# Forming the weight sums of seven-product passes later, from stored halves, and for passes of both layers

## The chip, the core and the metric

The kernel runs on one core of a Trainium2 chip. The metric is the device time of one execution, in microseconds; the median of several executions stands for a kernel. TensorE multiplies, VectorE, ScalarE and GpSimd do the rest, SyncE issues every DMA of the program from one queue in order.

## The reference

Block-causal attention over 4 x 8 heads of 576 positions and 64 columns, then two feed-forward layers on 2304 tokens of 512 columns, with 2048 inner columns:

```python
def reference(q, k, v, moe_w_in, moe_w_out, moe2_w_in, moe2_w_out):
    scores = np.where(block_i >= block_j, q @ k.T / sqrt(64), -1e9)   # blocks of 64
    x = softmax(scores) @ v                                            # to 2304 x 512
    h = x @ moe_w_in
    x = (h * tanh(softplus(h))) @ moe_w_out                            # mish, layer 0
    h = np.maximum(x @ moe2_w_in, 0.0)
    return (h * h) @ moe2_w_out                                        # layer 1
```

## The kernel before

Tokens are cut into six chunks of 384 columns (CH1). A chunk goes through attention, then through layer 0 and layer 1; one chunk through one layer is a pass, written (layer, chunk). PASSES gives their order: (0,0), (0,1), (0,2), (1,0), (1,1), (0,3), (1,2), (1,3), (0,4), (0,5), (1,4), (1,5), numbered 0 to 11. Attention of chunks 2 to 5 runs beside passes 0 to 7. Pass (0,0) multiplies in fp32. All others multiply f16 halves: a value is split into a high and a low f16 part, and a product takes three matmuls (high by high, low by high, high by low).

A pass has eight blocks j of 256 inner columns, two half blocks f each. `first_half` is a plain block's first product: per f four products of 384 columns into a bank hp, then an activation with a table function. `first_seven` does the same block with seven products of 128 x 256 by half the tokens instead of eight, Strassen's scheme: its weights are three blocks as they are and four sums or differences of blocks, its tokens are summed by `chunk_scale`'s `later` (L1238), and the results are put together on VectorE (L1325 to L1333). Before, all six passes of layer 1 run `first_seven`, all of layer 0 `first_half` (or `first_full` for (0,0)). `g_parts` then splits the activated block into halves, and `second_half` multiplies it by the second weights into four accumulators; it runs one block later, mixed with the next block's first products.

Weights arrive as raw 64-bit words and are decoded (`decode`), measured (`weigh`, L1127 and the matmul L1130) and split into f16 halves (`split`) on the chip. Layer 0's first weights stay in SBUF (`here`); all others are spilled to DRAM and fetched again for each pass (`weights`). For layer 1 that happens in passes (0,1) and (0,2): 16 units, eight of them first weights, which `sums` (L1163) turns into seven blocks and stores in sspill, 896 KB a block. A fetched block lies in a ring of three: "w7" for layer 1's first weights, "wl" for second weights from pass 3 on ("ws" before that). All these lie in one region, arena, and `follow` lists which ring may begin after which other one is done.

The order of all work is not worked out when the kernel is built: PLAN is a packed list of task numbers and engines, and `planned` issues the tasks in that order. Each engine keeps to it; between engines semaphores decide. A task that may run on several engines (`choose`, `copy`, `parts`) goes where the list says. Unpacked, the list before has 4601 tasks.

```python
    R["w7"] = fixed([seven(arena[:, 1792 * i:1792 * i + 1792]) for i in range(3)])
    R["wl"] = fixed([pair(arena[:, 5376 + 1024 * i:6400 + 1024 * i]) for i in range(3)])
...
    for o, a, b, op in ((3, 2, 3, ALU.add), (2, 0, 2, ALU.subtract), (0, 3, 0, ALU.subtract), (1, 1, 0, ALU.subtract)):
```

Of the kernel before, what the change touches and what calls it, by code (L numbers as in the profile page):

```python
# [16 lines left out]
F16 = mybir.dt.float16  # L17
# [7 lines left out]
DM = 512  # L25
# [39 lines left out]
def seg_len(tiles):  # L65
# [34 lines left out]
    "cIyP`BO7(2_Qi9X(cxj)sy*=UW*sdzNi8#l`|EY0T+flCn;5@Eua;?e<OZo=HsGW692Ly(+C?tK_GNkrBd(Pt8k;UMlz3huL*x-Tz>FpOkX#~vvGxkxFAvCN"  # L100
    "vJe~d<vdxSkIPp14sFko`B-ku2A+MbKWbz7L2sA2x=!XX?|%74dlT7(`j!5qU+T*`m!pOZlJE5d`ANPdKJ#^!)|9XD^+NfOZ1_RG(D(IwnT<C;)VK9cvS1e4"
    "&c^c}kvW~@6a9dQSnVi3;{RKT=SMPwtb0x0mv{6v?aDimx8x0diFjY5FH1*xPkZ72XY~qsLEqFvI)m#ejC&KGJ}n2ys62f|3(@denWpE<qeOqBj@RdiM1LJi"
    "raYumI5v?x7fUW)AE$rn1yaxasrM3*d$hSch|gA%8Gp+0X0!~{2XweBmHXvPa(boq)xYF6xkq1-TXZ3DT_9cMd$~iu(>rv4enY&LYA5Z3PjXBT`AUA)TV%G("
    "lPh$#bl1!EBWX?E-GFuN<Xyc=K9+an0_m(TNNMdzCJvRW^=f@XCrMNJK>w@Lh~f&ar=jof@~}K34P+udc~zg0mO4`IBO@Qzr-*6;nJf$BIc+aba@AI@k*WFu"
    "nRBsB<~%_kr4mQUH}V)UJ5R<?9b<H)j@8G_NEs%PJR~Dzl#V9$BV~(>z`_xn?~}pY-J@^FSRKl!(K<w?$i1w1Jb7Nky}R++B)MBE${?;DB`faKTjdEEAm!vS"
    ">CZ~HOMe|f=Jl4II*jvm5}8r5T5r{E*!!v6BR7&`S1Z}Bx8R$1r6sFgL*(v4`@7^y-gVIq(vSM@q@DE~^CEI@r1HN4m7bC&GF5s|e`iPsJyY5uwZ1IYHu@p?"
    "+Ekio6X{02eXVE7g-B_k&B(*)<nMVphP>}6&9uCkOGaIwjnT6yc|4q>y*x!loDIgDN6gNZbG4?PD;LVmtk;917HF0+^|c}K8_hazqjgtoJ5`TIi?gLbs&lsk"
    "qX%%OiNuV&RL+uWpjCgZCD~dIbUj`w$Zq*q2c!K>dJ`)gwy{<uHZA2;eEvIrE3{|f-G+Fmq70*UdLpfWds&ii8_Q`_PXjV=KN5D>+EQ2YwX@Wde%c%SI#rI7"
    ")8z`uH|uSIUM^ehu^{+%Q$v>96UmZla+TDSrFNM;PA;N;s>_wS!?c%d@}si+U~}|WdyHfl_k+ENY-q^+g|-pZaK0|Er&2Y|@xxFu=ni>C_v%OXpnhlvNs-N?"
    "4hNAV1$H2)Td0+Y{21vA%H4v^b4@SlOeM`W<)jyRa;r=LAA6GR|LF6a*XvD^V<*^$Wi7Sxi0y*bBV@eYK)qfgkDIHhV0T<ecHC#LkiT`2`Bon^^X)GnV|!Vr"  # L110
    "vvq{&17>g1|FCMVUPOJb(x2@pvmVxJA$OQR^j*6~KiBinWWC-4n!axT)VcO9(-4oYgh2)(w>{W7omJb(BCut-eqfjBH2s@;{7h#s{y8GG3{<Qpui54x@E2e~"
    "Yx9dfM{Iu4vq3$Frc>>Y#OEEIZ0GA+VC7Hxg#8*Me1jZ))K-*9U||CpYnw`6Q(t<S)5*}<=0x)$YmTrd$!X?fIYDZgQ)Q?<ftc2U7j8DMV#igSr%{PD;oq+2"
    "GE<RQjf0=2>eFPJiZM@7C9hH~3wgZ{_J5IxP2l~B;QAiUQ}I{}KYzQOO=j-X&$OATj_vtGZ6?e;lv-Mb9k-hIK=pTZ5UBnRHf+)*vRqCwZ)h+5O^QJ6%2LkM"
    "Fvo#c6+q4MR8@ig0xJDVmi{V><XUXbgGVR9nw97|D$2{nk5QT5>euqR&V{irrWV)0xO3zs?&ZSS`NZvS-GwGaps0WttPAJ<3v)h3g?tDeejpp*v18?3DyIw)"
    "dr23`3>gWcJ_m~|pgM=+li6_UWPKe^{HBe_w7DS1G&1WEodp{2hJBw!lZUu^gApyFd0@~cR=J-_+MxI1r(wkV9$4oCT@9|SqHbR&xAx(Yx52Q-;ebEj_^n9n"
# [459 lines left out]
def tile_attention_moe(ctx, tc, qk, qp, va, vd, w1, w2, out):  # L575
# [38 lines left out]
    R = {}  # L614
# [854 lines left out]
    def scale(l, c, m, at, first=False):  # L1469
# [12 lines left out]
        if l == 0:  # L1482
            due.append([NDELAY[l], l, c, norm, rest])
# [241 lines left out]
```

## Time and profile before

| | us |
|---|---|
| median of 3 runs (lowest, highest) | 924.68 (922.96, 926.22) |
| profiled execution | 930.72 |
| its span, first to last instruction | 928.9 |
| TensorE, VectorE, ScalarE, GpSimd busy | 886.9, 684.6, 535.3, 90.2 |
| TensorE's mean granted clock, share of full speed | 0.987 |
| read from and written to HBM, MB | 144.17, 20.45 |

Busy times are unions of instruction times. A matmul's end is modelled, so its busy time says little of its pace; starts are exact. All rows are in us from the span's start, except means marked ns.

### The profile page before, as it was taken

To read this page: it belongs to the slowest core of one execution; us is meant where nothing else is said; L and a number is where in the kernel's file an instruction comes from. 1 tells how busy PE (TensorE), PEld (TensorE's weight loads), DVE (VectorE), ACT (ScalarE), POOL (GpSimd) and SP (SyncE) were. 2 spreads that over 40 slices of the span, in tenths; PEclk is the share of its full clock that TensorE was granted. 3 is DMA by queue.
4 is the path that set the end of the run, shared out by engine and by line. 5 is a ranking of instruction groups with operands and counts; after the bars stand their busy time and mean duration, and the time that the engine had idled before them with its cause. 6 is when DMAs were issued, how large, how long until landed. Compare 5 with 4: busy or idle time off the path is not lost.

```text
span 928.9 us, 17345 instructions
## 1 busy us (share of the span) xinstructions
PE 886.9 (95%) x6650; PEld 589.4 (63%) x6650; DVE 684.6 (74%) x1697; ACT 535.3 (58%) x1003; POOL 90.2 (10%) x102
## 2 busy tenths in 40 slices
PE   7999999888899799999999899999999999999998
PEld 6665555544455377767655467777766666787775
DVE  5989999999899999989899678775531333376433
ACT  5898896889899685676556444643332222233421
POOL 1000100020111001311010010001110010011010
PEclk8999999999999999999999999999999999999999
DMA  9896469889899998799936594887541222246562
GB/s 351 339 353 228 123 137 250 200 279 333 247 302 244 251 306 242 185 279 286 214 90 157 148 220 168 232 222 241 179 151 49 89 68 77 103 162 227 209 207 73
DMA packets 141779, 190.92 MB, mean 206 GB/s; under 512 B 105856, under 2 KB 110976, under 8 KB 141696
## 3 DMA queue, kind: packets, MB, share of 16 engines
q1 hardware_dynamic: 141696, 189.81, 67.5%
q8 instruction: 52, 0.85, 0.4%
q14 instruction: 31, 0.25, 0.1%
HBM read 144.17 MB, written 20.45 MB: 177 GB/s over the span
## 4 chain that ended last, share of the span: by engine, by line
PE 61%; DVE 19%; DMA 9%; ACT 7%; issue 2%; SPq 1%; POOL 0%; ACTq 0%; DVEq 0%
PE acc L1393 24%; PE hp L1315 13%; PE hp L1295 9%; PE hp L1348 4%; PE acc L1362 4%; DVE pb L783 2%; DVE st L883 2%; DMA arena<-wspill 2%; DMA pt<-pb 2%; ACT pad L894 2%; DVE arena L783 2%; PE bank L872 2%; PE bank L980 2%; DVE g L783 1%; DMA wspill<-arena 1%
## 5 line engine op out<-in xcount | busy, mean ns | idle before, releaser
L1393 PE MATMUL acc<-g,arena 128*128 128x384 f16 x2112 | 406.8, 327 | 6.2 <-DMA arena<-wspill 6.0
L1393 PEld LDWEIGHTS <-arena 128*128 128x128 f16 x2112 | 200.4, 98 | 124.4 <-issue 13.1
L1315 PEld LDWEIGHTS <-arena 128*128 128x128 f16 x2016 | 172.4, 98 | 31.8 <-issue 6.1
L1295 PE MATMUL hp<-xt,first 128*128 128x384 f16 x768 | 149.0, 330 | 2.8 <-ACT h L1300 2.6
L783 DVE SCALAR_TENSOR_TENSOR g<-h,cst,g 128x768 f16<-128x768 f32 x88 | 89.1, 1013 | 66.0 <-ACT g L1085 39.4
L1295 PEld LDWEIGHTS <-first 128*128 128x128 f16 x960 | 92.9, 98 | 70.0 <-issue 11.7
L1315 PE MATMUL hp<-xt,arena 128*128 128x192 f16 x1008 | 103.0, 247 | 2.9 <-DVE first L1325 2.2
L1315 PE MATMUL hp<-arena 128*128 128x192 f16 x1008 | 101.6, 248 | 0.8 <-DVE h L1328 0.3
L1300 ACT ACTIVATE h<-hp,cst 128x384 f32<-128x384 f32 x80 | 45.1, 576 | 82.1 <-PE hp L1295 81.9
L894 ACT ACTIVATE pad<-bank,st,sq 128x448 f32<-128x448 f32 (+1 forms) x96 | 65.3, 682 | 26.0 <-DVE st L888 21.4
L783 DVE SCALAR_TENSOR_TENSOR pb<-pad,st,pb 128x512 f16<-128x512 f32 (+2 forms) x96 | 71.8, 753 | 2.8 <-ACT pb L914 2.6
L1335 ACT ACTIVATE h<-h,cst 128x576 f32<-128x576 f32 x48 | 37.0, 770 | 60.8 <-DVE h L1333 60.7
L1086 POOL TENSOR_SCALAR g<-h,cst 128x768 f16<-128x768 f32 x34 | 32.4, 953 | 338.1 <-PE acc L1393 174.2
L883 DVE TENSOR_REDUCE st<-bank 128x1 f32<-128x448 f32 (+1 forms) x96 | 53.2, 571 | 5.8 <-PE bank L875 3.2
L1085 ACT ACTIVATE g<-h,cst 128x768 f16<-128x768 f32 x42 | 39.0, 929 | 27.8 <-PE acc L1393 23.4
L1331 ACT ACTIVATE h<-hp,cst 128x192 f32<-128x192 f32 x48 | 20.0, 417 | 59.1 <-PE hp L1315 52.8
L914 ACT ACTIVATE pb<-pad,st 128x384 f16<-128x384 f32 (+2 forms) x66 | 46.5, 712 | 11.9 <-DVE st L906 5.0
L1348 PE MATMUL hp<-xs,first 128*128 128x384 f32 x128 | 48.7, 494 | 0.0
L1333 DVE TENSOR_TENSOR h<-first,hp 128x384 f32<-128x384 f32 x48 | 26.4, 550 | 28.4 <-PE hp L1315 28.4
L872 PE MATMUL bank<-q 64*128 64x448 f16 (+2 forms) x384 | 40.2, 306 | 4.0 <-ACT xs L994 1.4
L1362 PE MATMUL acc<-h,late 128*128 128x384 f32 x96 | 37.6, 495 | 0.0
L1295 PE MATMUL hp<-xs,first 128*128 128x384 f16 x192 | 36.8, 326 | 0.0
(255 smaller groups left out, 1221.8 us busy)
## 6 DMA issues: line engine op xcount, KB each, us to landing
arena<-wspill SPq DMA_DIRECT2D x88, 512.0 KB, 4.3
arena<-sspill SPq DMA_DIRECT2D x48, 896.0 KB, 5.6
arena<-in_w_dram SPq DMA_DIRECT2D x27, 1023.8 KB, 6.8
wspill<-arena SPq DMA_DIRECT2D x16, 512.0 KB, 3.4
qk<-in_qp_dram SPq DMA_DIRECT2D x16, 480.0 KB, 5.2
sspill<-arena SPq DMA_DIRECT2D x8, 896.0 KB, 4.5
vs<-in_va_dram SPq DMA_DIRECT2D x16, 320.0 KB, 4.6
pad<-in_w_dram SPq DMA_DIRECT2D x5, 1023.8 KB, 5.7
```

The source lines that it names most:

```text
L783: return sch.add("DVE", c_dve(n) + 62 * ap, lambda: nc.vector.scalar_tensor_tensor(dst(), a(), s() if ap else s, c(), op0, op1), r=r, w=w, ...
L872: nc.tensor.matmul(out=pp.t[hd][:, o:o + k1 - k0], lhsT=qh.t[rows, u, a:a + 128], rhs=qh.t[rows, w, nq + k0:nq + k1], start=p == 0, stop=p ...
L883: t = sch.add("DVE", c_dve(o1 - o0), lambda hd=hd: nc.vector.reduce_max(st.t[:, 2 * j + hd:2 * j + hd + 1], pp.t[hd][:, o0:o1], axis=AX.X) ...
L894: t = sch.add("ACT", c_act(o1 - o0, True, 3), lambda hd=hd: nc.scalar.activation(pf[hd].t[r0:, k0:k0 + o1 - o0], view(hd)[r0:, o0:o1], AF. ...
L914: "ACT": ("ACT", c_act(n, False, 1), lambda pb=pb, pv=pv, s=s: nc.scalar.activation(pb.t[:, 0:i + 1, 0, :], pv(), AF.Copy, scale=s()), False),
L1085: "ACT": ("ACT", c_act(n, False, 1), lambda: nc.scalar.activation(dst(0), src(), AF.Copy, scale=s()), False),
L1295: nc.tensor.matmul(out=hp.t[:, 0:n], lhsT=w.t[:, f % 2, a, 128 * k:128 * k + 128], rhs=x.t[:, c, k, 0:n], start=k == 0 and i == 0, stop=k ...
L1300: sch.add("ACT", c_act(n, True, 1), lambda f=f, o=o, hp=hp: nc.scalar.activation(h.t[:, o * n:o * n + n], hp.t[:, 0:n], AF.Mish, scale=cst ...
L1315: nc.tensor.matmul(out=bank.t[:, o:o + z], lhsT=w.t[:, a, b, 128 * k:128 * k + 128], rhs=x.t[:, c, ks[k], :], start=start and k == 0 and i ...
L1348: nc.tensor.matmul(out=hp.t[:, 0:n], lhsT=wf.t[:, 512 * (f % 2) + 128 * k:512 * (f % 2) + 128 * k + 128], rhs=xs.t[:, k, 0:n], start=k == ...
L1362: ts.append(sch.add("PE", c_mm(4 * n), lambda m=m, acc=acc: nc.tensor.matmul(out=acc.t[:, 0:n], lhsT=wf.t[:, 512 * (f % 2) + 128 * m:512 * ...
L1393: nc.tensor.matmul(out=acc.t[:, 0:n], lhsT=wo.t[:, f % 2, a, 128 * m:128 * m + 128], rhs=g.t[:, c, f % 2 * n:f % 2 * n + n], start=f == 0 ...
```

## The change

`sums` and its store of seven blocks go. Layer 1's first weights are split as all others and stored as halves, 512 KB a block. A new function `upgrade` reads a block's halves, adds them (1024 wide, f16 and f16 to f32), forms the four sums, makes f16 halves of these and stores them in uspill (512 KB). It runs 16 times: during pass 5 for layer 1 (it fetches the halves for that, eight loads more) and during pass 7 for layer 0, whose halves lie in SBUF. `first_seven` takes its three plain blocks from the ordinary weights and the four sums from a second load (`sums_of`, ring "w4"). SEVEN names the six passes that use it: (1,2), (1,3), (0,4), (0,5), (1,4), (1,5). Passes (1,0) and (1,1) become plain (`first_half`, now with Relu and a square for layer 1). First and second weights of layer 1's passes share the ring "wl" of three. Slots of token tiles (X_AT) and the `follow` rules are adapted.

```
+SEVEN = {(1, 2), (1, 3), (0, 4), (0, 5), (1, 4), (1, 5)}
+UP = {5: [(1, j) for j in range(8)], 7: [(0, j) for j in range(8)]}
...
-    R["w7"] = fixed([seven(arena[:, 1792 * i:1792 * i + 1792]) for i in range(3)])
-    R["wl"] = fixed([pair(arena[:, 5376 + 1024 * i:6400 + 1024 * i]) for i in range(3)])
+    R["wl"] = fixed([pair(arena[:, 1024 * i:1024 * i + 1024]) for i in range(3)])
+    R["w4"] = fixed([four(arena[:, 3072 + 1024 * i:4096 + 1024 * i]) for i in range(3)])
+    R["un"] = fixed([four(arena[:, 6144:7168])])
+    R["uw"] = fixed([arena[:, 7168:8192]])
...
+    def upgrade(pi, l, j):
+        w = weights(pi, l, 0, 2 * j)
+        q, u = R["uw"].new(), R["un"].new()
+        sch.add("DVE", c_dve(1024), lambda: nc.vector.tensor_tensor(q.t..., w.t[:, :, 0, :], w.t[:, :, 1, :], ALU.add), r=both, w=[q], lock=True)
+        for o, x, y, op in ((3, 2, 3, ALU.add), (2, 0, 2, ALU.subtract), (0, 3, 0, ALU.subtract), (1, 1, 0, ALU.subtract)):
+            sch.add("DVE", c_dve(256), lambda ...: nc.vector.tensor_tensor(b(o), b(x), b(y), op), w=[q], lock=True)
+        copy(ENG["wh"], 1024, lambda: u.t[:, 0], qv, [q], [(u, 0)])
+        sub(V, 1024, lambda: u.t[:, 1], qv, lambda: u.t[:, 0], [q, (u, 0)], [(u, 1)])
+        dma(lambda: nc.sync.dma_start(uspill[l, j]..., u.t), 128 * 4096, r=[u], w=[ud[l, j]])
+
+    def sums_of(l, j):
+        s = R["w4"].new()
+        dma(lambda: nc.sync.dma_start(s.t, uspill[l, j]...), 128 * 4096, r=[ud[l, j]], w=[s])
...
-            if (l, k) == (1, 0):
-                w = fetched[pi, l, k, j] = R["w7"].new()
...
+            w = fetched[pi, l, k, j] = R["wl" if pi >= WL_AT else "ws"].new()
...
-            m1, h = (first_seven if l else first_half)(pi, l, j, n, x, cst)
+            for i in range(len(ups) * j // (NF // 2), len(ups) * (j + 1) // (NF // 2)):
+                upgrade(pi, *ups[i])
+            m1, h = (first_seven if (l, c) in SEVEN else first_half)(pi, l, j, n, x, cst)
```

PLAN is replaced as a whole. Unpacked, the new list has 4721 tasks, with TensorE steps as many as before (1690), VectorE steps 1734 for 1691, ScalarE 763 for 749, GpSimd 86 for 95, SyncE 448 for 376. Where VectorE's steps stand in it, counted between the first matmuls of successive passes:

| VectorE steps | 0 | 1 | 2 | 3 | 4 | 5 | 6 | 7 | 8 | 9 | 10 | 11 |
|---|---|---|---|---|---|---|---|---|---|---|---|---|
| pass | (0,0) | (0,1) | (0,2) | (1,0) | (1,1) | (0,3) | (1,2) | (1,3) | (0,4) | (0,5) | (1,4) | (1,5) |
| before | 306 | 247 | 207 | 169 | 181 | 162 | 131 | 73 | 33 | 44 | 79 | 59 |
| after | 311 | 178 | 152 | 170 | 159 | 143 | 200 | 119 | 84 | 78 | 82 | 58 |
| attention's, before | 235 | 145 | 81 | 101 | 115 | 125 | 47 | 8 | | | | |
| attention's, after | 239 | 101 | 68 | 120 | 125 | 54 | 122 | 16 | | | | |
| upgrades', after | | | | | | 50 | 6 | 29 | 12 | | | |

## Rows read from the trace of the kernel before

**Rows 1.** Busy time by stage: start:end, length, then per engine; clock, DMA share, GB/s
```profile
0.00:132.20 132.20, 125.25 (x605) 79.42 (x605) 114.28 (x309) 108.57 (x252) 8.68 (x18) 0.97 0.75 261
132.20:326.10 193.90, 169.14 (x1158) 94.66 (x1151) 182.26 (x459) 164.19 (x273) 22.09 (x25) 0.98 0.90 259
326.10:547.70 221.60, 215.36 (x1865) 145.00 (x1866) 195.83 (x510) 138.64 (x274) 26.89 (x27) 0.98 0.80 214
...
547.70:673.60 125.90, 125.31 (x1154) 96.88 (x1153) 87.96 (x207) 52.73 (x93) 11.86 (x11) 1.00 0.68 205
673.60:798.80 125.20, 125.20 (x774) 75.36 (x771) 38.26 (x77) 31.79 (x49) 11.05 (x12) 1.00 0.25 84
798.80:928.90 130.10, 126.64 (x1110) 98.04 (x1108) 66.02 (x138) 39.42 (x64) 9.65 (x9) 1.00 0.48 171
...
326.10:387.60 61.50, 60.77 (x593) 46.16 (x594) 59.61 (x169) 40.96 (x84) 10.65 (x12) 0.98 0.84 240
```

**Rows 2.** Chain of work in order of time: start, us, engine, tile, line, count
```profile
113.49 1.29 PE hp L1348 x4
...
794.09 1.46 PE hp L1295 x9
...
798.96 0.49 PE hp L1315 x6
```

**Rows 3.** Timeline of VectorE near 203 us: start, us, instruction
```profile
203.10 1.21 DVE L1115 SCALAR_TENSOR_TENSOR arena<-arena 128x1024 uint32<-128x1024 uint32 x1
204.23 0.74 DVE L1087 TENSOR_SCALAR arena<-arena,us 128x1024 f16<-128x1024 f32 x1
```

**Rows 4.** Waits of TensorE, whole run: total us, times, longest us
```profile
PE bank L1130 <- ACT wsq L1127: 8.8, 8, 2.2
PE acc L1393 <- DMA arena<-wspill: 6.0, 3, 2.3
```

**Rows 5.** Groups by line and shape: count, busy us, mean ns of one, idle before
```profile
L783 DVE SCALAR_TENSOR_TENSOR arena<-arena,us 128x512 f16<-128x512 f32 x8 | 6.0, 747 | 1.7 <-ACT arena L1085 1.6
L783 DVE SCALAR_TENSOR_TENSOR arena<-arena,us 128x256 f16<-128x256 f32 x8 | 3.8, 478 | 0.4 <-ACT arena L1085 0.3
L1085 ACT ACTIVATE arena<-arena,us 128x1024 f16<-128x1024 f32 x13 | 14.8, 1142 | 5.1 <-DVE arena L1175 2.4 <-DMA sspill<-arena 1.8 <-DMA wspill<-arena 0.9
L1115 DVE SCALAR_TENSOR_TENSOR arena<-arena 128x1024 uint32<-128x1024 uint32 x16 | 19.4, 1215 | 0.0
L1175 DVE TENSOR_TENSOR arena<-arena 128x256 f32<-128x256 f32 x32 | 13.4, 418 | 0.1
L1255 DVE TENSOR_TENSOR nsq<-nsq,wsq 128x768 bf16<-128x768 bf16 x11 | 6.0, 550 | 0.0
L1325 DVE TENSOR_TENSOR first<-first,hp 128x192 f32<-128x192 f32 x48 | 16.8, 349 | 15.9 <-ACT first L759 15.2
L1327 DVE TENSOR_TENSOR h<-first,hp 128x192 f32<-128x192 f32 x48 | 16.9, 352 | 19.5 <-PE hp L1315 18.1
L1333 DVE TENSOR_TENSOR h<-first,hp 128x384 f32<-128x384 f32 x48 | 26.4, 550 | 28.4 <-PE hp L1315 28.4
L1340 DVE TENSOR_TENSOR h<-h 128x768 f32<-128x768 f32 x11 | 11.1, 1006 | 4.1 <-ACT h L1335 4.1
```

**Rows 6.** Second-weight loads from 673.6, 798.8, 547.7, 326.1 us on; last line: min/median/max
```profile
arena<-wspill SPq DMA_DIRECT2D x16, 512.0 KB, 3.2
...
arena<-wspill SPq DMA_DIRECT2D x16, 512.0 KB, 3.8
...
arena<-wspill SPq DMA_DIRECT2D x16, 512.0 KB, 4.3
...
arena<-wspill SPq DMA_DIRECT2D x22, 512.0 KB, 4.7
...
DMA to landing us min/median/max: 3.1/4.3/9.4
```

**Rows 7.** Waits of SyncE's queue, whole run: total us, times, longest us
```profile
SPq L919 <- DVE pb L783: 53.9, 22, 8.8
```

More of the change, by code (lines that the diff above doesn't have):

```diff
@@ L100 @@
[L100 to L103, printed above, removed]
@@ L180 @@
[L180 to L183 removed]
+    "c-mE(2cQ&1^8c%62OgORNKT5FJp@nC6Gag)p%_q65D`VhQ}j^8@Dmd%2J}Qd#EfDDNh(SZ3}huplAOZ>$?5T8*Z<SqGmC$Q-JPB3uCA`|{Z{Qf5hK;)L}@9N"
@@ L617, in tile_attention_moe @@
     pair = lambda t: t.bitcast(F16).rearrange("p (a f c) -> p f a c", f=2, a=2)
-    seven = lambda t: t.bitcast(F16).rearrange("p (a b c) -> p a b c", a=2, b=7)
+    four = lambda t: t.bitcast(F16).rearrange("p (a b c) -> p a b c", a=2, b=4)
     wsl = arena[:, 0:1024 * NWS]
@@ L1182, in unit @@
         us = weigh(l, k, [j], [wf], at)
-        return sums(j, wf, us) if k == 0 else split(l, k, j, wf, us, 0)
+        return split(l, k, j, wf, us, 0)
     fetched = {}
@@ L1213, in tile_attention_moe, with chunk_scale @@
     PX, SX, CI, CF, T0, HS, GS = 0, 1, 2, 3, 4, 5, 21
-    def chunk_scale(l, xs, xm, x, n, m, at, first):
+    def chunk_scale(l, xs, xm, x, n, m, at, first, seven):
         cst, sc = (R[k].new() for k in ("cst", "sx"))
@@ L1226, in chunk_scale @@
         flip(lambda: c(PX), lambda: c(SX), [(cst, PX)], [(cst, SX)], 1)
-        for k in range(KC if l == 0 else 0):
+        for k in range(0 if seven else KC):
             parts(ENG["xh"], n, lambda s, k=k: x.t[:, s, k, 0:n], lambda k=k: xs.t[:, k, 0:n], lambda: c(SX), xs, (cst, SX), x, k)
@@ L1247, in norm @@
             for k, sq, v in zip(range(0, KC, 2), sqs, view):
-                if l == 0:
+                if not seven:
                     sch.add("ACT", c_act(2 * n), lambda k=k, v=v: nc.scalar.activation(v(), x.t[:, 0, k:k + 2, 0:n], AF.Square),
@@ L1300, in first_half, with square @@
             sch.add("ACT", c_act(n, True, 1), lambda f=f, o=o, hp=hp: nc.scalar.activation(
-                h.t[:, o * n:o * n + n], hp.t[:, 0:n], AF.Mish, scale=cst.t[:, HS + f:HS + f + 1]),
-                    r=[(cst, (HS, f // 2))], w=[hp, (h, o)], table="mish")
+                h.t[:, o * n:o * n + n], hp.t[:, 0:n], (AF.Mish, AF.Relu)[l], scale=cst.t[:, HS + f:HS + f + 1]),
+                    r=[(cst, (HS, f // 2))], w=[hp, (h, o)], table=("mish", None)[l])
+        if l:
+            square(n, h)
         return ts, h
+    def square(n, h):
+        hv = lambda: h.t[:, :]
+        choose(ENG["sq"], {
+            "ACT": ("ACT", c_act(2 * n), lambda: nc.scalar.activation(hv(), hv(), AF.Square), False),
+            "POOL": ("POOL", c_pool(2 * n), lambda: nc.gpsimd.tensor_tensor(hv(), hv(), hv(), ALU.mult), False),
+            "DVE": ("DVE", c_dve(2 * n), lambda: nc.vector.tensor_tensor(hv(), hv(), hv(), ALU.mult), True)}, [], [h])
     def first_seven(pi, l, j, n, x, cst):
         w = weights(pi, l, 0, 2 * j)
+        s = sums_of(l, j)
         p, q = R["hp"].new(), R["hp"].new()
@@ L1470, in scale @@
         sch.group = "scale", l, c
-        x = (summed if l else halved)(X_AT[l, c])
-        x, cst, norm, spread, rest, later = chunk_scale(l, *source[l, c], x, n, m, at, first)
+        seven = (l, c) in SEVEN
+        x = (summed if seven else halved)(X_AT[l, c])
+        x, cst, norm, spread, rest, later = chunk_scale(l, *source[l, c], x, n, m, at, first, seven)
         if l == 0:
             spread()
-        else:
+        if l or seven:
             sch.group = "norm", l, c
             norm()
+            if l == 0:
+                rest()
+        if seven:
             sch.group = "scale", l, c
@@ L1481, in scale @@
         ready[l, c] = x, cst, spread, rest
-        if l == 0:
+        if l == 0 and not seven:
             due.append([NDELAY[l], l, c, norm, rest])
@@ L1557, in tile_attention_moe @@
         units = list(UNITS.get(pi, ()))
+        ups = UP.get(pi, ())
         base = clock
```

242 lines of the change are left out of this document (120 added, 122 removed).

## Prediction

> **What bounds the kernel now.** I read the stage table first [rows 1]. It cuts the run at the starts of passes, the matmul runs of one chunk through one layer: A, attention's beginning and the fp32 pass (0,0); B, passes (0,1), (0,2); C, passes (1,0), (1,1), (0,3); D, (1,2), (1,3); E, (0,4), (0,5); F, (1,4), (1,5). TensorE is busy 886.9 of 928.9 us, but a matmul's busy time stretches while the next waits, so I measure a need instead: each form's count in a stage times the spacing of its starts where nothing waits. Nine 384-column matmuls take 1.46 us, 162.5 ns each; six of 192 columns 0.49 us, 82.5 ns; four fp32 halves 1.29 us, 323 ns [rows 2]; attention's matmuls get a full-clock cycle per column, half that where two row groups run side by side. Needs in A to F: 106.7, 153.0, 199.6, 123.7, 125.1, 126.3 us. Stage E, with no attention, is long by 0.1 us against its need, so the yardstick holds. Together 834.4: the run loses 94.5 us, 25.5 in A, 40.9 in B, 22.0 in C, 2.2 in D, 0.1 in E, 3.8 in F.
>
> VectorE's load is the sum of its instructions less 0.08 us each, by which one starts before the last ends: L1115 begins at 203.10, takes 1.21, and the next begins at 204.23 [rows 3]. Its loads in A to F: 112, 178.9, 190.7, 81.5, 34.5, 59.7 us. Load over TensorE's need: B 1.17, C 0.955, D 0.66, E 0.28. Stage B is bound by VectorE (busy 182.3 of 193.9), with ScalarE behind it (164.2); TensorE waits there mostly for ScalarE, L1130 for the squares of L1127 above all, 8.8 us, every one of these waits in B [rows 4]. In C both are nearly full. In E TensorE alone counts. So the loss follows that quotient: 27% of TensorE's need at 1.17, 11% at 0.955, 1.8% at 0.66, 0.1% at 0.28.
>
> **The change, part by part.** Six passes have seven products before and after, so TensorE's total need stays. A plain pass is 384 x 162.5 ns = 62.4 us, one with seven products 336 x 82.5 + 192 x 162.5 = 58.9 us [rows 2]; (1,0) and (1,1) get 3.5 us longer each, (0,4) and (0,5) shorter.
>
> Sums, removed from B: per unit four 256-wide operations (418 ns), a 512-wide and a 256-wide low half (747, 478 ns) [rows 5]; less 0.08 each, 2.4 us, 19.4 for eight units. ScalarE loses 8 us of high halves, and the store shrinks from 896 to 512 KB. Nothing else hides these: VectorE is B's bound.
>
> Seven products, moved: a block costs VectorE three 192-wide operations (349 to 352 ns, L1325 to L1328) and a 384-wide one (550 ns) [rows 5], less overlap 1.28 us, 20.5 us for 16 blocks. They leave C, where they compete with attention, and go to E, where VectorE is busy 38.3 of 125.2 us [rows 1]: no cost there.
>
> Upgrades, added: 16 times a 1024-wide add, four 256-wide operations, a copy, a 1024-wide subtract and a store. No row shows a 1024-wide add of two f16 into f32. L1115 at 1024 (1215 ns) bounds it from above; L1255, all 16 bit, takes 550 ns for 768, which gives about 0.73 us below [rows 5]. I take 1.2, since its output is f32 and L1340, all f32, takes 1006 ns for the same 768; the lower end would save 16 x 0.5 = 8 us of VectorE work, nowhere on the bound for more than a few. So 1.14 + 4 x 0.34 + 1.14 = 3.6 us each, 58 us in all, about 2 more for the copies that VectorE takes; the others are 1.14 us on ScalarE [rows 5].
>
> The order decides where this lands, and the new list moves much else. From its steps per pass, each with the duration of the same step in the trace: VectorE in B -39.7 us (sums -23 with high halves, attention -17, which goes later); C -3.7 (seven products -20.7, upgrades +30.8, attention -17.3, chunk scales and others the rest); D +44.6 (attention +26.7, upgrades +20.6); E +34.6 (seven products +22.3, upgrades +7.2); A and F within 2. TensorE's needs become 110.3, 144.3, 203.9, 131.8, 118.2, 125.7. Quotients: B 0.965, C 0.917, D 0.957, E 0.585. ScalarE gets 35 us lighter in B; exp and mish alternate 8 times less in (0,3), since attention's last chunk runs beside a Relu pass.
>
> Losses by the quotients of before: A 25.5 as it is; B 11%, 15.9; C 10%, 20.4; D 9%, 11.9 (its half (1,3) is at 0.89); E 1.4; F 3.9. Sum 79.0 against 94.5: **15.5 us** less.
>
> The ring, a cost that the diff doesn't speak of: first and second weights of layer 1's passes now share three buffers of 512 KB; before they had three each. In the old order at least 7 and mostly 10 to 20 us of matmuls stand between the last reader of a buffer and the first reader of its next content; in the new one 4.9 to 6 in F and D's tighter loads, 5 to 10 in C. The 512 KB load lands in 3.2 us (median) in E, 3.8 in F, 4.3 in D, 4.7 in C, at worst 9.4 after its issue [rows 6]. So margins of 10 us become margins of one, in 96 loads, and behind each wait of SyncE's queue stand the loads and attention's transposes after it; TensorE waits for them. Taking before's landings with these margins, F loses 0.18 us a load, D and C between 0 (margin 6.5) and 0.4 to 0.8 (margin 5): 0 to 44 us. Before's first-weight loads were 896 KB and delayed their neighbours, so I take the lower half: **8 us**. The 48 loads of sums have 11 us or more of margin; those in E cost nothing at 84 GB/s, the 8 extra loads and 16 stores delay only what is queued behind.
>
> The Trainium skill (DMA: Bandwidth & Descriptors, Anatomy of one DMA) gives a load, for the path from GpSimd, a fixed 2.0 us and its bytes over 436 GB/s. For 512 KB that is an estimated 3.2 us, and E's lone loads, though issued by SyncE, take 3.2 [rows 6]. By that rule alone no load would miss even the 4.9 us margin, the ring would be free and the sum 8 us lower; C's 4.7 us shows what other traffic adds.
>
> Sum on the profiled execution: 928.9 - 15.5 + 8 = 921.4 us span; 1.8 us lie around it (930.72). That execution is 6.0 us above the median 924.68, so the median should come to **917 us**.
>
> **Rivals.** *The relief is larger.* If B without its bound loses 7% (10.1), C 8%, D 5% and loads behave as in E, losses fall to 64 us: 928.9 - 31 + 1.8 - 6.0 = 894. For it: ScalarE's waits [rows 4] vanish with its load. Against: C loses 11% with ScalarE no fuller than that.
>
> *The bound travels.* VectorE's total grows by 38 us, and attention's last chunk with six upgrade steps now sits in (1,2), 73 us of VectorE on 72 of TensorE. If that pass loses 27% as B did (19.5), and C 25 us because upgrades share (0,3) with attention, the gain is gone: 925, no change. For it: in C VectorE is busy 88%. Against: (1,0) had 58.3 us of VectorE on 56.0 before, 1.04, and lost 10%, not 27% [rows 1].
>
> *The ring decides, slower.* Every block of the six passes of layer 1 waits for its loads. With margins of 6 us in C and D the landings of before give 18 + 6 + 6 = 30 us: 928.9 - 15.5 + 30 + 1.8 - 6.0 = 939. It decides from 15.5/96 = 0.16 us per load. For it: 22 loads in C have a median of 4.7 [rows 6], and SyncE is in order, so a transpose waiting for VectorE (53.9 us in 22 waits before) [rows 7] holds the weights behind it. Against: where TensorE is late anyway, margins widen by as much.
>
> **How the numbers follow.** Forecast 0.43, larger relief 0.20, travelling bound 0.17, ring 0.20. The likeliest is 917, by itself 908 to 926. For 8 in 10 the range reaches half into either side: 897 to 935; upgrades at their lower price and ring costs from 0 to 30 lie within. A measurement of this kernel tells 0.3% from no change, 2.8 us. Faster: 0.37 of the forecast, the relief, and 0.04 of the travelling bound, 0.61. Same: 0.04 + 0.10, 0.14. Slower: the rest, 0.25.
>
> **What would show it.** Right: B shrinks from 193.9 to about 160 us with VectorE under 90% busy, C is within 10 us of its old length, (1,2) grows by some 12, E falls to 118 to 120. Wrong, by the ring: waits of TensorE for arena loads of tens of us in passes of layer 1, in F too, where nothing else is short; before they are 6.0 us in all [rows 4]. Wrong, by the travelling bound: VectorE over 93% busy in (0,3) and (1,2), with TensorE waiting there for exp or for L1325 to L1333. Wrong, by misjudging B: B as long as its quotient allows but TensorE still waiting for L1127.

## The result, and the profile after

The changed kernel takes 894.8 us (median; 894.0 to 895.7) against 923.8 of the kernel before beside it: ratio 0.968, 95% interval 0.966 to 0.971, 29 us faster. Forecast were 917 us in a range from 897 to 935: the direction was right, the time lies 2 us below the range, and the first rival, *the relief is larger*, had 894. The profiled execution took 894.7 us, its span is 892.9.

The stage table of the changed kernel, columns as in [rows 1], stages A to F cut at the same passes:

```profile
0.00:135.50 135.50, 127.85 (x630) 81.13 (x631) 115.66 (x313) 115.56 (x264) 6.52 (x17) 0.99 0.83 277
135.50:291.10 155.60, 152.47 (x1057) 89.51 (x1056) 143.88 (x334) 128.47 (x208) 25.58 (x27) 1.00 0.87 249
291.10:505.70 214.60, 212.65 (x1526) 123.80 (x1526) 194.60 (x473) 129.10 (x242) 15.25 (x17) 1.00 0.85 228
505.70:644.70 139.00, 136.37 (x1278) 101.42 (x1276) 130.95 (x320) 89.70 (x170) 13.16 (x14) 1.00 0.95 257
644.70:762.80 118.10, 118.10 (x1060) 93.19 (x1059) 77.17 (x163) 37.82 (x61) 9.58 (x9) 1.00 0.47 167
762.80:892.90 130.10, 126.04 (x1108) 97.72 (x1105) 69.83 (x140) 38.39 (x66) 8.16 (x9) 1.00 0.58 200
```

Against [rows 1], B is 38 us shorter, C and E 7 each; D is 13 longer, since attention's last chunk and upgrades now sit there. With TensorE's need measured by the prediction's yardstick, the stages compare like this (us):

| | A | B | C | D | E | F | sum |
|---|---|---|---|---|---|---|---|
| need, forecast | 110.3 | 144.3 | 203.9 | 131.8 | 118.2 | 125.7 | 834.2 |
| need, measured | 109.9 | 145.5 | 204.8 | 130.3 | 118.2 | 125.8 | 834.5 |
| VectorE's load over need, forecast | | 0.965 | 0.917 | 0.957 | 0.585 | | |
| the same, measured | | 0.969 | 0.923 | 0.976 | 0.605 | | |
| lost, before | 25.5 | 40.9 | 22.0 | 2.2 | 0.1 | 3.8 | 94.5 |
| lost, forecast without the ring | 25.5 | 15.9 | 20.4 | 11.9 | 1.4 | 3.9 | 79.0 |
| lost, measured | 25.5 | 10.1 | 9.8 | 8.7 | 0.0 | 4.3 | 58.4 |

Needs came out within 1.2% and quotients within 4%. What failed is the step from the load to the loss, and the size of the ring's cost. Single passes show the step most plainly: pass (0,3) of the kernel before, then (0,3) and (1,2) of the changed one:

```profile
469.00:547.70 78.70, 76.20 (x528) 42.94 (x527) 63.64 (x160) 47.54 (x86) 7.04 (x8) 0.98 0.62 159
436.70:505.70 69.00, 68.36 (x474) 40.78 (x472) 67.31 (x144) 40.96 (x64) 1.81 (x2) 1.00 0.89 266
505.70:581.30 75.60, 75.04 (x705) 53.94 (x703) 73.43 (x201) 57.11 (x121) 9.57 (x10) 1.00 1.01 253
```

Their needs by the same yardstick are 70.9, 66.8 and 70.5 us. Before, (0,3) had VectorE busy 81% of the time and lost 7.8 us; now VectorE is busy 98% of it and it loses 2.2. (1,2), at 97%, loses 5.1, and TensorE's listed waits in these two passes of the changed kernel sum to 1.1 us, 0.3 of them for the putting together of products and none for exp; the rest of their losses stands in no listed wait. VectorE above 93% in both was one half of the prediction's sign for the travelling bound; the other half, TensorE waiting there for exp or the products, shows with those 0.3 us only.

TensorE's waits of the changed kernel, whole run (total us, times, longest), four of them:

```profile
PE hp L1304 <- ACT h L1309: 1.4, 4, 0.5
PE hp L1304 <- DMA arena<-wspill: 0.7, 1, 0.7
PE hp L1335 <- DMA arena<-wspill: 0.6, 1, 0.6
PE acc L1411 <- DMA arena<-wspill: 0.4, 2, 0.2
```

The 8.8 us for the squares of a weight unit [rows 4] have no successor: the waits listed for stage B sum to 3.1 us, and none is for them. The waits for weight loads are 1.7 us in all, where they were 6.0 before [rows 4] and the prediction added 8 for the ring.

The upgrades' groups by line and shape (count, busy us, mean ns, idle before):

```profile
L771 DVE TENSOR_TENSOR arena<-arena 128x1024 f16<-128x1024 f32 x16 | 19.5, 1219 | 0.9 <-ACT arena L764 0.8
L1177 DVE TENSOR_TENSOR arena<-first 128x1024 f32<-128x1024 f16 x8 | 9.7, 1218 | 0.0
L1177 DVE TENSOR_TENSOR arena<-arena 128x1024 f32<-128x1024 f16 x8 | 9.7, 1218 | 0.0
```

The wide add that no row of before showed (L1177) takes 1.22 us; of the two bounds (0.73 and 1.2) the upper one, which was taken, was right.

### The profile page after: what moved, and what is told of

Read it like the earlier page. It is cut to its first block, busy times and chain, and to the rows that moved or that the text cites. A ratio compares the mean times of both kernels' runs of the same rounds, so it can differ in the third digit from the quotient of the medians.

```text
span 892.9 us, 17533 instructions
## 1 busy us (share of the span) xinstructions
PE 873.5 (98%) x6650; PEld 586.8 (66%) x6650; DVE 732.1 (82%) x1740; ACT 539.0 (60%) x1009; POOL 78.3 (9%) x93
## 4 chain that ended last, share of the span: by engine, by line
PE 71%; DVE 14%; DMA 7%; ACT 4%; issue 2%; SPq 0%; POOL 0%; ACTq 0%; DVEq 0%; POOLq 0%
PE acc L1411 29%; PE hp L1335 15%; PE hp L1304 13%; PE hp L1366 3%; PE acc L1380 3%; PE bank L877 2%; DVE pb L788 2%; DMA pt<-pb 2%; PE bank L985 2%; DVE st L888 2%; DMA late<-pb 1%; DMA arena<-wspill 1%; DVE g L788 1%; DVE pb L920 1%; DVE arena L788 1%
## 5 line engine op out<-in xcount | busy, mean ns | idle before, releaser
L1411 PE MATMUL acc<-g,arena 128*128 128x384 f16 x2112 | 398.8, 326 | 1.1 <-ACT late L1424 0.7
L1411 PEld LDWEIGHTS <-arena 128*128 128x128 f16 x2112 | 200.3, 98 | 114.0 <-issue 4.3
L1335 PEld LDWEIGHTS <-arena 128*128 128x128 f16 x1728 | 146.8, 98 | 21.3 <-issue 1.5
L1304 PE MATMUL hp<-xt,first 128*128 128x384 f16 x576 | 109.4, 326 | 1.4 <-ACT h L1309 1.0
L788 DVE SCALAR_TENSOR_TENSOR g<-h,cst,g 128x768 f16<-128x768 f32 x88 | 90.5, 1028 | 20.4 <-ACT g L1090 10.7
L1335 PE MATMUL hp<-arena 128*128 128x192 f16 x864 | 85.8, 246 | 0.3 <-DVE h L1348 0.3
L1335 PE MATMUL hp<-xt,arena 128*128 128x192 f16 x864 | 84.5, 246 | 0.9 <-DMA arena<-wspill 0.6
L1304 PEld LDWEIGHTS <-first 128*128 128x128 f16 x576 | 55.1, 98 | 39.7 <-issue 4.3
L788 DVE SCALAR_TENSOR_TENSOR pb<-pad,st,pb 128x384 f16<-128x384 f32 (+2 forms) x96 | 72.4, 763 | 7.3 <-ACT pb L919 7.0
L1304 PE MATMUL hp<-xt,arena 128*128 128x384 f16 x384 | 72.6, 326 | 1.1 <-DMA arena<-wspill 0.7
L919 ACT ACTIVATE pb<-pad,st 128x512 f16<-128x512 f32 (+2 forms) x70 | 49.5, 714 | 13.5 <-DMA pt<-pb 4.0
L1304 PEld LDWEIGHTS <-arena 128*128 128x128 f16 x384 | 36.4, 98 | 26.7 <-issue 1.9
L1090 ACT ACTIVATE g<-h,cst 128x768 f16<-128x768 f32 x34 | 31.7, 932 | 13.9 <-PE acc L1411 5.6
```

The lines of the kernel that those rows point to most:

```text
L788: return sch.add("DVE", c_dve(n) + 62 * ap, lambda: nc.vector.scalar_tensor_tensor(dst(), a(), s() if ap else s, c(), op0, op1), r=r, w=w, ...
L919: "ACT": ("ACT", c_act(n, False, 1), lambda pb=pb, pv=pv, s=s: nc.scalar.activation(pb.t[:, 0:i + 1, 0, :], pv(), AF.Copy, scale=s()), False),
L1304: nc.tensor.matmul(out=hp.t[:, 0:n], lhsT=w.t[:, f % 2, a, 128 * k:128 * k + 128], rhs=x.t[:, c, k, 0:n], start=k == 0 and i == 0, stop=k ...
L1335: nc.tensor.matmul(out=bank.t[:, o:o + z], lhsT=lhs, rhs=x.t[:, c, ks[k], :], start=start and k == 0 and i == 0, stop=k == 1 and i == 2, s ...
L1411: nc.tensor.matmul(out=acc.t[:, 0:n], lhsT=wo.t[:, f % 2, a, 128 * m:128 * m + 128], rhs=g.t[:, c, f % 2 * n:f % 2 * n + n], start=f == 0 ...
```

## Experiments under the old list: work taken out

Three theories stand against each other. *L*, the prediction's: a stage's loss follows VectorE's load. *S*: in B TensorE waits for ScalarE. *K*: in C the chain within a block counts, not the load. If one of them is the whole story, then the kernel before must get faster when that work is left out of it. In the four kernels of this section the tasks left out keep their places in the list but issue nothing. The pieces are a unit's two plain parts, 512 and 256 wide.

```
-    sch.add("DVE", c_dve(256), lambda ...: nc.vector.tensor_tensor(q(o), q(a), q(b), op), w=[wf], lock=True)
+    sch.add("DVE", c_dve(256), lambda: None, w=[wf], lock=True)          # b_sums_dve_out, b_both
...
+        if j:
+            mute(t for t in sch.tasks[begin:] if t.opts)                 # b_sums_act_out, high halves of two pieces
...
+        if pi in (3, 4):                                                 # b_c_dve_out, b_both
+            mute(t for t in sch.tasks[begin:] if t.eng == "DVE" and not t.opts)
```

> The kernel before with one thing left out: of `sums`, the four 256-wide VectorE operations that form the sums and differences of a block (32 in all, 13.4 us of VectorE in passes (0,1) and (0,2)); the last four of the seven blocks are then plain blocks. Theory L (the loss of a stage follows VectorE's load, the rule of the prediction): stage B's load falls from 178.9 to 168, its quotient from 1.17 to 1.10, its loss from 40.9 to 33: 7 to 8 us faster. Theory S (in stage B TensorE waits for ScalarE, and VectorE only lengthens that chain): ScalarE's queue stays as full as it was, 0 to 4 us faster.

> The kernel before with one thing left out: for seven of the eight first-weight units of layer 1, the high halves of the 512-wide and of the 256-wide piece in `sums`, which ScalarE makes in 12 of the 14 cases (about 7.3 us of ScalarE and 1 us of VectorE); the low halves are then taken against stale values. Theory L: VectorE's load hardly changes, 0 to 2 us faster. Theory S: it takes off the engine that TensorE waits for, 4 to 10 us faster, and the waits of TensorE for L1127 get shorter.

> The kernel before with one thing left out: in passes (1,0) and (1,1) the four VectorE operations that put the seven products of a block together (L1325, L1327, L1328, L1333; 1.28 us a block net of overlap, 20.5 us in 16 blocks); the activation reads three copies of one product from the bank instead. Theory L: stage C's quotient falls from 0.955 to 0.853 and its loss from 22.0 to 15.6: 6 us faster. Theory K (in C TensorE waits for the chain bank, VectorE, ScalarE, next bank, not for VectorE's load): the loss falls to what the changed kernel shows in C, about 10, of which 4.4 are the half-clock spells that go away with the waits: 10 to 14 us faster.

> The kernel before with both left out: the 32 sums in stage B (as in the first kernel of this group) and the putting together of the products in passes (1,0) and (1,1) (as in the third). Both stages' gains should add: by theory L 7.5 + 6.4 = 14 us, by theories S and K 2 + 12 = 14 us. The total does not tell the theories apart, the stages do: L wants half of it in B, S and K nearly all in C. If the total is well under the sum of the two single kernels, one stage only handed its wait to the next.

| left out of the kernel before | median us | ratio to it | 95% interval |
|---|---|---|---|
| 32 sums (VectorE, B) | 923.0 | 1.0007 | 0.9974 to 1.0040 |
| high halves of two pieces (ScalarE, B) | 923.2 | 0.9991 | 0.9970 to 1.0012 |
| putting products together (VectorE, C) | 923.9 | 0.9991 | 0.9971 to 1.0011 |
| sums and putting together | 923.5 | 0.9978 | 0.9954 to 1.0002 |

Not one of the four is faster by an amount that can be told from none, though the last one lacks 30 us of VectorE's work. S allowed that for the first kernel and L for the second; no theory allowed it for the last two. Its stages B and C:

```profile
131.20:323.60 192.40, 168.84 (x1153) 94.43 (x1151) 171.89 (x427) 164.10 (x274) 22.05 (x25) 0.98 0.90 263
323.60:542.70 219.10, 213.64 (x1866) 145.29 (x1865) 175.86 (x446) 137.75 (x274) 25.59 (x27) 0.98 0.82 215
```

VectorE is busy 10 us less in B and 20 us less in C than in [rows 1], and the stages stand nearly as they were: 1.5 and 2.5 us shorter. Executions differ by more: the one of [rows 1] lies 7 us above its kernel's median, and B shows 190.2 us in the kernel that leaves work out in C alone and 187.1 in the one without high halves, whose medians are those of the kernel before. Stage C here, with VectorE busy 175.9 of 219.1 us, loses 19.5 us; the changed kernel's C, with VectorE busy 194.6 of 214.6, loses 9.8. So load alone does not set the loss.

Why nothing is gained is suggested by the chain of work in stage B (followed back from the run's last instruction, at each step to what released it), by line, first of the kernel before, then of the kernel with both left out:

```profile
by line: DVE arena L783 7.5%; ACT pad L894 7.1%; DMA arena<-wspill 6.7%; DMA wspill<-arena 6.0%; issue 5.4%; DMA pt<-pb 5.2%; PE acc L1362 4.6%; DVE st L883 3.8%; PE hp L1295 3.8%; DVE arena L1115 3.4%; PE acc L1393 3.3%; ACT h L1300 3.3%; 
```

```profile
by line: issue 8.0%; ACT pad L894 7.7%; PE hp L1300 7.5%; DVE arena L783 6.6%; DMA pt<-pb 5.3%; ACT arena L1085 4.8%; PE acc L1371 4.6%; ACT wsq L1132 4.5%; DMA wspill<-arena 4.5%; ACT L894 3.7%; ACT h L1305 3.6%; DVE st L883 3.5%; DMA aren
```

No line has a tenth of it. Summed over its pieces, the chain of before spends 58 us on VectorE, 47 on ScalarE, 43 in DMAs and 32 on TensorE; with the work gone 54, 62, 29 and 32. The path runs on through ScalarE and through waits of nearly the same length. Each engine works through its part of the list in order, so a hole in one engine's work can turn into a wait for the next entry's input; that it does so here is read from the chain, and no run tests it by itself. The Trainium skill says of the queues that ScalarE's, VectorE's and GpSimd's are strict first in, first out (PSUM — Partial Sum Buffer, Engine vs sequencer instructions); 30 us of holes worth nothing are in keeping with it. The same row of the changed kernel's stage B:

```profile
by line: PE hp L1304 27.3%; PE acc L1411 25.2%; PE bank L877 4.3%; DMA arena<-in_w_dram 4.1%; PE acc L1380 4.1%; issue 3.8%; DVE arena L788 3.3%; ACT pad L899 2.7%; ACT arena L1118 2.6%; DVE pb L788 1.4%; ACT wsq L1132 1.4%; PE bank L985 1.
```

Here over half is TensorE's own products.

## Experiments on the changed kernel: work put in or left out

Idle work, on a spare tile and read by nobody, is issued behind a task that is there already; and the arithmetic of upgrades is left out. The list stays the new one.

```
+    spare = first[:, 16384:17152].bitcast(F32)
+            lo[0].fn = lambda: (old(), dummy(256, 256, 256, 256, 384, 384))   # a_b_load, VectorE; a_b_act: ScalarE, five of 384
...
+                low.fn = lambda: (old(), dummy(192, 192, 192, 384))           # a_c_load, behind each block's g in (1,0), (1,1)
...
+        if j:
+            mute(t for t in sch.tasks[begin:])                                # a_up_out
```

> The changed kernel with idle work added: per first-weight unit of layer 1 (eight, in passes (0,1) and (0,2)) four 256-wide and two 384-wide VectorE operations on a spare tile, about 2.8 us a unit, 22 us of VectorE, right behind the unit's low half; nothing reads their result. Theory L (loss follows VectorE's load): stage B's load goes from 139 to about 158 on a need of 145.5, quotient 1.08, loss about 20% or 29 us in place of 10: 15 to 20 us slower. Theory S (TensorE waits for ScalarE there): 0 to 6 us slower.

> The changed kernel with idle work added: at the same eight places, five 384-wide copies on ScalarE in place, about 3 us a unit, 24 us of ScalarE (128.5 of 155.6 us busy in stage B without them); nothing reads them. Theory L: VectorE's load is unchanged, 0 to 4 us slower. Theory S: ScalarE is then as full as it was before the change, 10 to 20 us slower, with TensorE waiting for the squares of L1132 and the exp of L899.

> The changed kernel with idle work added: in passes (1,0) and (1,1), behind the low half of each block's g, three 192-wide and one 384-wide VectorE operation on a spare tile, the sizes that seven products need there, 20.5 us in 16 blocks, but off the chain of the block; nothing reads them. VectorE is busy 194.6 of 214.6 us in stage C without them. Theory L: as much lost as seven products cost before, 8 to 14 us slower. Theory K (the chain counts, not the load): 0 to 5 us slower.

> The changed kernel with the arithmetic of 14 of the 16 upgrades left out (all but the first of each layer): the wide add, the four sums, the copy and the subtract, about 3.6 us of VectorE and 1.1 of ScalarE each, 50 us of VectorE in all, most of it in passes (0,3) to (0,4); the stores and loads stay, of stale values. Theory L: quotients of C and D fall by 0.1 to 0.2, their losses (9.8 and 8.7) by about 10 us: 8 to 12 us faster. Theory K: upgrades stand off every chain and fill gaps of VectorE, 0 to 4 us faster.

Medians: 918.1 (ratio to the kernel before 0.992, 0.990 to 0.995), 909.1 (0.984, 0.978 to 0.990), 908.5 (0.982, 0.977 to 0.987) and 895.8 us (0.968, 0.963 to 0.973). Stage B with VectorE's idle work, then with ScalarE's, then stage C of the third kernel:

```profile
135.30:310.90 175.60, 157.41 (x1058) 90.36 (x1057) 162.92 (x376) 128.93 (x208) 25.51 (x27) 0.98 0.77 221
```

```profile
133.50:304.90 171.40, 156.22 (x1056) 90.14 (x1055) 143.23 (x334) 145.22 (x243) 24.35 (x27) 0.98 0.78 226
```

```profile
290.40:518.20 227.80, 216.91 (x1526) 124.07 (x1526) 216.74 (x536) 129.64 (x242) 15.18 (x18) 1.00 0.81 214
```

VectorE gets 19.0 us more to do in B and the stage 20.0 us longer; ScalarE 16.7 more and the stage 15.8. Both are paid nearly in full. Each theory's forecast held, within 4 us, for the engine it names and failed for the other one, so neither engine is the bound alone. In C 22.1 us more cost 13.2, off any chain of a block: against K, which allowed 5. Upgrades' arithmetic, 26 us of VectorE less in C and 18 in D, brings nothing, as K had it and as the holes under the old list did. In stage C of one and the same list, then, 22 us of VectorE's work put in cost 13, and 26 us left out return nothing.

## Experiments with new lists

If that is so, work that leaves is worth something only to a list that is made anew. The file still has a planner that works out an order from costs; with PLAN empty it runs, with the same settings for each kernel. Work that is left out has a cost of almost nothing in the planner's eyes too.

```
-PLAN = ("c-mE...
+PLAN = ""
...
-            t.fn, t.opts = none, tuple((o[0], o[1], none, o[3]) for o in t.opts)
+            t.dur, t.fn, t.opts = 1.0, none, tuple((o[0], 1.0, none, o[3]) for o in t.opts)
...
-SEVEN = {(1, 2), (1, 3), (0, 4), (0, 5), (1, 4), (1, 5)}                      # a_own_four
+SEVEN = {(1, 2), (1, 3), (1, 4), (1, 5)}
```

> The kernel before with the packed list taken out: the order comes from the planner that stands in the file (due times and costs built in), all work as before. A yardstick for the three runs beside it, which get their order in the same way: 0 to 6% slower than the kernel before, since the packed list differs from the planner's in most places. No theory is at stake in it alone.

> The changed kernel with its packed list taken out, order from the same planner with the same settings. Theory R (the change of structure gives the gain, and a new list is what cashes it): 20 to 40 us below the kernel before with the planner's order, as with the packed lists (29). Theory P (the new packed list is simply a better arranged one, the structure matters little): within 10 us of it.

> The kernel before with the planner's order, and with the two kinds of VectorE work left out that brought nothing under the old list: the 32 sums in passes (0,1), (0,2) and the putting together of products in passes (1,0), (1,1); the planner knows that they cost nothing. Theory R (under a fixed list other chains keep the old pace; a new list can use the room): 10 to 20 us below the kernel before with the planner's order. Rival N (this work was never what the stages wait for): within 4 us of it.

> The changed kernel with the planner's order and only layer 1's four late passes with seven products: (0,4) and (0,5) are plain, and the eight upgrades of layer 0 are left out with them. TensorE's need is 2 x 3.5 = 7.0 us more, VectorE has some 48 us less to do in passes (1,3) to (0,5). Theory E (layer 0's seven products lie where VectorE has room, and pay their 7 us in full): 5 to 8 us above the changed kernel with the planner's order. Rival: their upgrades and joins cost in (1,3) and E what they save: within 2 us.

> The kernel before with the planner's order and without the 32 sums in passes (0,1), (0,2), which the planner knows to cost nothing. With them 1010.8 us; without them and without the putting together of products 991.7. Theory L (stage B is bound by VectorE's load, 10.8 us of it are sums): 8 to 13 us below 1010.8, and all of that in stage B. Theory K (the seven products' work in stage C is what the new list can use): 1 to 6 us below.

> The kernel before with the planner's order and without the putting together of products in passes (1,0), (1,1), which the planner knows to cost nothing (20.5 us of VectorE net of overlap). Theory L as the prediction applied it (quotient in C from 0.955 to 0.853): 5 to 8 us below 1010.8. Theory K: 12 to 18 us below, most of it in stage C. The two single gains should add to 19 us if the stages don't share a wait.

> The changed kernel with the planner's order, and the arithmetic of 14 of the 16 upgrades left out (50 us of VectorE, 16 of ScalarE or its substitutes; stores and loads stay, of stale values), which the planner knows to cost nothing. Theory G (upgrades run in gaps that no list can use otherwise): 0 to 4 us below 975.5. Theory L: stages C and D are loaded by them, 8 to 15 us below.

> The kernel before with the planner's order, without the 32 sums and, in seven of eight first-weight units, without the high and low halves of the 512-wide and 256-wide pieces (VectorE 8.6 us, ScalarE 8 us more than the sums); the store of seven blocks keeps its size, with stale values. Theory L (stage B is paid by work on VectorE and ScalarE): the sums gave 16.1 us for 10.8 us net of VectorE work; 18 us net then give 24 to 30 us below 1010.8. Rival Q (only the four sums in a row count, since the pieces run while others wait): 14 to 19 us below.

> The same, and without the putting together of products in passes (1,0), (1,1). Theory L: 3 to 6 us less than the run beside it, so 27 to 36 us below 1010.8, what the changed kernel has with the planner's order (975.5). Rival Q: 17 to 23 us below.

| with the planner's list | median us | against its yardstick | ratio to the kernel before, 95% interval |
|---|---|---|---|
| kernel before | 1010.8 | | 1.0889 to 1.0973 |
| without the putting together in C | 1006.2 | -4.6 | 1.0863 to 1.0942 |
| without sums | 994.7 | -16.1 | 1.0721 to 1.0810 |
| without both | 991.7 | -19.2 | 1.0701 to 1.0759 |
| without sums and small pieces | 983.8 | -27.0 | 1.0591 to 1.0714 |
| without sums, small pieces, putting together | 983.7 | -27.1 | 1.0594 to 1.0713 |
| changed kernel | 975.5 | -35.4 | 1.0527 to 1.0587 |
| changed, four passes with seven products | 980.3 | +4.9 to the changed | 1.0562 to 1.0636 |
| changed, without upgrades' arithmetic | 967.9 | -7.5 to the changed | 1.0451 to 1.0515 |

Both kernels are 9% slower with these lists than with their packed ones (0 to 6% was expected), but the change is worth 0.965 between them, as between the packed ones (0.968): the gain belongs to the structure, and not to one list. The rows come from three sets of runs, beside which the kernel before took 921.6 to 924.3 us, so a difference between sets is uncertain by 2 or 3 us. Sums and small pieces give 27 of the 35 us (26 by the ratios). They were 13.4 us of sums [rows 5] and some 16 more of the two engines: under a new list, a microsecond of either engine off these units is worth about one. The sums alone gave 16, more than either theory allowed (8 to 13, or 1 to 6). The putting together of seven products, 20 us of VectorE, gives 4.6, inside the intervals and less than either theory's (5 to 8, or 12 to 18), and nothing on top of the pieces. The difference of 4.9 for layer 0's seven products agrees with their 7 us, but the intervals overlap. Upgrades cost 7.5, which is 0.15 for each of their 50 us, between the two theories.

Stages B and C of the kernel before, of the one without sums and pieces, and of the changed one, all with the planner's list:

```profile
143.30:348.40 205.10, 161.83 (x1052) 89.25 (x1050) 187.49 (x438) 133.93 (x216) 25.64 (x25) 0.90 0.75 219
348.40:607.80 259.40, 230.49 (x1954) 152.87 (x1955) 226.55 (x585) 150.08 (x289) 14.30 (x15) 0.95 0.76 198
```

```profile
139.60:329.90 190.30, 155.83 (x1022) 90.20 (x1020) 172.61 (x384) 117.01 (x193) 26.49 (x26) 0.92 0.81 240
329.90:572.80 242.90, 221.65 (x1886) 148.58 (x1882) 211.10 (x546) 138.11 (x257) 10.98 (x13) 0.99 0.78 202
```

```profile
145.10:321.70 176.60, 154.46 (x1021) 88.17 (x1020) 165.13 (x378) 115.06 (x191) 25.14 (x26) 0.94 0.79 233
321.70:550.80 229.10, 218.98 (x1565) 125.51 (x1563) 195.23 (x462) 129.74 (x231) 17.70 (x16) 1.00 0.76 210
```

In the second pair C has lost 16 us of its length although nothing of C's own work is left out: the list moved other work out of it (VectorE there 211 for 227 us). The packed lists differ in the same way. Attention's exponentials by stage are 43, 62, 8 in B, C, D before, and 32, 50, 30 after: D, where VectorE was busy 88 of 126 us [rows 1], takes what B and C no longer have to hold.

One planner's list scatters against the next by several us (with work left out in C alone, B came out 11 us longer), so single steps under 5 us in the table say little.

## The ring

```
+            more = lambda: nc.sync.dma_start(scrap[pi - 10, k, j], wspill[l][k, j]) if pi >= 10 else None
+            dma(lambda: (more(), nc.sync.dma_start(flat4(w.t), spill(l, k, j))), 128 * 4096, r=[wd[l, k, j]], w=[w])
```

> The changed kernel (its own packed list) with a copy of 512 KB from DRAM to DRAM issued ahead of each of the 32 weight loads of passes (1,4) and (1,5); nothing reads the copies. They delay each load by the time of 1 MB of traffic, 2 to 3 us as the 4.1 us landings in D against 3.2 for lone loads let expect. Theory T (margins of 4.9 to 6 us as read from the list, landings of 3.7): loads then land after 5.5 to 7 us, 0.5 to 1.5 us late each, stage F 10 to 40 us longer. Rival W (loads are called for far ahead of their matmuls, real margins are twice that): stage F at most 4 us longer.

902.9 us, ratio to the kernel before 0.978 (0.974 to 0.982). Stage F, then its loads (KB each, median us from issue to landing), then TensorE's waits in it:

```profile
761.30:899.30 138.00, 127.76 (x1107) 96.82 (x1105) 69.87 (x140) 38.27 (x66) 8.14 (x9) 1.00 0.83 306
```

```profile
arena<-wspill SPq DMA_DIRECT2D x32, 512.0 KB, 5.2
```

```profile
PE hp L1337 <- DMA arena<-wspill: 3.3, 5, 1.5
PE acc L1413 <- DMA arena<-wspill: 2.8, 4, 1.4
```

In the changed kernel, where no wait of TensorE for a load is listed in F, the same loads take this long, then those in D and C:

```profile
arena<-wspill SPq DMA_DIRECT2D x32, 512.0 KB, 3.7
arena<-wspill SPq DMA_DIRECT2D x30, 512.0 KB, 4.1
arena<-wspill SPq DMA_DIRECT2D x46, 512.0 KB, 4.3
```

Landings rose by 1.5 us in the median and the stage by 7.9, just under what theory T named (10), twice what rival W allowed. The nine waits are for loads that landed 5.0 to 7.8 us after their issue; landing less wait gives 4.7 to 5.7 us for eight of them. So the margins of 4.9 to 6 us were read rightly: at a median of 3.7 us no load misses them by a listed wait, at 5.2 nine do. The ring is free in F as long as loads land as they do, and 1.5 us more make it cost.

## Why the prediction was wrong

**Needs, loads, durations**: right. The ScalarE waits for the squares went, B came to 156 us (160 forecast), (1,2) grew by 10.7 us (12), E is 118.1. One sign missed: VectorE is busy 92% of B, not under 90.

**The loss from the quotient**, that a stage's loss follows VectorE's load over TensorE's need, is the step that failed: 21 of the 28.5 us by which the span was missed (B 5.8, C 10.6, D 3.2, E 1.4); the other 8 were set for the ring, whose waits lie within the measured losses. Forecast were 11, 10 and 9% of need in B, C and D; measured 6.9, 4.8 and 6.7. Above 0.66 the rule had two points, B at 1.17 and C at 0.955 of before, and it took the loss there for a function of load. Even the kernel before does not follow it pass by pass: by the same yardstick (1,0), (1,1) and (0,3) have quotients of 1.03, 0.98 and 0.86 and lose 10, 13 and 11% of their need. The runs under the old list deny it too: with 10 and 20 us of load gone from B and C the losses stay at 39 and 19.5. So the 11% at 0.955 belonged to that list, which left D with three tenths of VectorE's time idle; part of it was the clock (below). The changed kernel's own list loses 4.8% at 0.92.

**The credit for the sums** came near in size, with too simple a reason. The prediction called VectorE B's bound and gave B a relief of 25 us for 40 us of load less; it was 31, and new lists give 27 over the whole run for sums and pieces alone. But idle work on ScalarE cost B about as much per microsecond as idle work on VectorE, so VectorE is not the bound by itself, and "Nothing else hides these" is false of the old list.

**The putting together moved to E**: no cost there, as said (E loses 0.0).

**The ring**: sized 8 us, measured 1.7, since loads land in 3.7 in F, 4.1 in D and 4.3 in C, most of them within the margin. By the rule that the Trainium skill gives for the path from GpSimd (DMA: Bandwidth & Descriptors, Anatomy of one DMA: a fixed 2.0 us and the bytes over 436 GB/s, an estimated 3.2 us for 512 KB) the ring should cost nothing. That is nearer to the 1.7 us than the forecast was, but the rule has no term for other traffic, which took the median to 5.2 us in the experiment.

**The profiled execution**: before's lay 6.0 us above the median, and the forecast took these off as a whole; the changed kernel's execution lies at its median, so 6 us of the span's miss don't show in the median's: 28.5 - 6 gives the 22 us. For the same reason the losses of before, from which all rates were taken, hold some 6 us that a median execution does not have. And the first rival owes its nearness in part to luck: it had losses of 64 us for 58.4 measured, with C too dear (8% for 4.8) and D too cheap (5 for 6.7), and the 6.0 us taken off made up for the rest.

**Still open**: what sets the loss instead of the load. No run divides C's further 10 us into attention moved to D, the clock and the easier blocks; the single steps are within the scatter of the lists.

## To carry to other kernels

Work taken out of a fixed order of instructions need not show what that work costs: four kernels with up to 30 us less stood still, and the same sums and putting together were worth 19 us once the order was made anew. So judge a change that brings its own order by needs and loads stage by stage, and take the loss rates of the old order for a first guess only: here they came out 3 to 11 us too high in B, C and D. For each shared buffer compare the margin with the landing under the traffic of that stage: here 1.5 us more in the landing made one stage 8 us longer.

## What the runs showed of the clock

Waits slow TensorE beyond their own length. Two stretches of the kernel before, columns as in [rows 1], then the matmul just ahead of the second one (start, us, instruction, and the idle time before it):

```profile
236.60:243.60 7.00, 4.73 (x32) 2.34 (x31) 5.13 (x11) 5.02 (x8) 0.00 (x0) 1.00 0.54 175
243.60:247.00 3.40, 3.40 (x13) 1.67 (x11) 3.32 (x15) 3.10 (x5) 1.86 (x2) 0.50 0.67 205
```

```profile
243.26 0.16 PE L1130 MATMUL bank<-us,onesq 128*128 128x1 bf16 x1 [2.14 <-ACT wsq L1127]
```

After the wait for the squares the granted clock is 0.50, the lower level of 1.2 GHz, for 3.4 us: the 384-column matmuls in it start 320 ns apart instead of 162. B and C of before have five such stretches, 17 us in all, and by the starts of their matmuls they cost TensorE about 8.5 us, half their length. The changed kernel has none there (clock 1.00 in both). With VectorE's idle work in B they are back (0.98), and with the planner's list the clock of stage B is 0.90 in the kernel before and 0.94 in the changed one. In the rows shown the engine had waited 2 us for its input before the clock fell. The prediction did not name this cost; it carried it on inside the loss rates of before. In C the stretches cost about 4.8 of the 22.0 us lost, which makes an estimated 4 to 5 of the 10.6 us by which the forecast for C was too high.
